# Loading the partial first and last blocks of x as a multiple of 16 rows and a rest

## The chip, the cores and the metric

The kernel runs on one core of one Trainium2 chip. The metric is the device time of one execution in microseconds (us). The spans in the profiles are some 1.7 us shorter than the device times of the same runs (445.9 against 447.63 for the kernel before).

## The reference

Two layers on x of 8 sequences x 4160 rows x 192 columns in float32: a causal convolution over 7 rows with softmax weights per head, then the channel mix of RWKV.

```python
def _attn_ref(x, weight):                       # x (8, 4160, 192), weight (8, 7)
    w = softmax(weight, axis=-1)                # cut: written out in the original
    x_pad = np.concatenate([np.zeros((B, 6, D)), x], axis=1)
    out = einsum('hk,bskhg->bshg', w, windows_of_7_rows(x_pad))
    return out.reshape(B, S, D)

def _moe_ref(x, mu_k, mu_r, w_k, w_v, w_r):     # w_k (192, 1024), w_v (1024, 192), w_r (192, 192)
    x_prev = x shifted down by one row
    xk = mu_k * x + (1.0 - mu_k) * x_prev
    xr = mu_r * x + (1.0 - mu_r) * x_prev
    k = np.maximum(xk @ w_k, 0.0)
    v = k * k @ w_v
    r = 1.0 / (1.0 + np.exp(-(xr @ w_r)))
    return r * v
```

## The kernel before

The rows of a sequence lie on the 128 partitions in blocks. A block gives 120 rows of output and needs 6 rows more ahead of them, so that one matmul with a banded 128x128 matrix (`toe`) is the convolution. `groups` says how many blocks are loaded at once. Two sequences (a pair) are worked on together, so a group is a tile `xb` of 128 partitions x blocks x 2 sequences x 192 columns.

```python
HALO = K - 1            # 6
BLK = 120
NBLK = -(-S // BLK)     # 35 blocks; the last has 86 rows of x
...
groups = []
for p in range(NPAIR):                      # 4 pairs of sequences
    blk0 = 0
    for nb, s, on_pe in (
        ((3, 0, True), (4, 1, True), (4, 2, True), (5, 3, True), (10, 4, False), (9, 6, False))
        if p == 0
        else ((10, 0, False), (10, 2, False), (10, 4, False), (5, 7, False))
    ):
        groups.append((p, blk0, nb, first_bundle[first_step[p] + s], on_pe))
        blk0 += nb
```

The first block of a sequence has no rows ahead of it: its 122 rows of x go to partitions 6 to 127, the other 6 hold zeros. The last block has 86 rows. Both are loaded by a DMA of their own, and the whole blocks of the group by a further one (the "main load" here). GpSimd (POOL) issues all of them, and they convert float32 to bfloat16 on the way.

```python
def load_x(g):
    p, blk0, nb, _, _ = groups[g]
    xb = xbs[g]
    for s in range(2):
        b = 2 * p + s
        lo, hi = 0, nb
        if blk0 == 0:
            lo = 1
            nc.gpsimd.dma_start(out=xb[HALO:P, 0, s, :], in_=x[b, 0 : P - HALO, :])
        t0 = blk0 * BLK - HALO
        if blk0 + nb == NBLK:
            hi = nb - 1
            r0 = t0 + hi * BLK
            nc.gpsimd.dma_start(out=xb[0 : S - r0, hi, s, :], in_=x[b, r0:S, :])
        nc.gpsimd.dma_start(
            out=xb[:, lo:hi, s, :],
            in_=bass.AP(
                tensor=x.tensor,
                offset=x.offset + (b * S + t0 + lo * BLK) * D,
                ap=[[D, P], [BLK * D, hi - lo], [1, D]],
            ),
        )
```

The start of the kernel, in the order in which POOL gets its work. The matrices `wk`, `wr` and `wv` are loaded by three, five and one DMAs.

```python
def prologue():
    ...
    load_x(0)          # group 0: two partial loads, two main loads
    masks_band()       # two short POOL instructions
    ...
    load_x(1)
    load_wk()
    load_x(2)
    load_wr()
    load_wv()
    ...
    for t in tails:
        nc.gpsimd.memset(t, 0.0)
    for c in range(0, len(chunks(0)), 2):
        conv_mm(0, c)  # the first convolution
    ...                # transposes of group 0, convolution of group 1
    x_tile(3, nc.vector)
    load_x(3)          # the fourth group
```

## Time and profile before

| what | kernel before |
|---|---|
| median of the first 3 runs | 447.46 us (447.34 to 447.76) |
| span in the profile | 445.9 us |
| TensorE busy | 433.8 us, 97% |
| POOL busy, instructions | 48.2 us, 70 |
| partial loads of x | 16: 8 of 122 rows, 8 of 86 rows |

The profiles call TensorE PE, VectorE DVE, ScalarE ACT, GpSimd POOL and SyncE SP. "Busy" is the time in which an engine works on an instruction; the chain of waits is the sequence of work, each piece released by the one ahead of it, that ended last. The prediction below shows the lines of the page and of the chain. The list of DMA queues of the kernel before gives packets, MB and the share of 16 engines:

```profile
q0 software_dynamic: 38224, 14.68, 29.1%
```

The timeline of TensorE gives start in us, length in us, engine, line, operation, output and inputs, shapes, count, and in brackets how long TensorE had been idle and what it waited for:

```profile
8.06 0.66 PE L250 MATMUL ps_c<-xb,toe 128*128 128x144 bf16 x8 [0.70 <-DMA xb<-in_x_dram]
...
23.82 0.98 PE L250 MATMUL ps_c<-xb,toe 128*128 128x240 bf16 x8 [1.20 <-DMA xb<-in_x_dram]
```

These are the two places where TensorE waits for x: the convolution of group 0 (3 blocks x 48 columns = 144) and that of the fourth group (5 blocks x 48 = 240). q0 is the queue of the DMAs that POOL issues.

### The profile page before, as it was taken

What the parts mean: (1) busy time and instruction counts of PE and PEld (TensorE: products, weight loads), DVE (VectorE), ACT (ScalarE), POOL (GpSimd) and SP (SyncE); (2) the same over time, 40 slices, a digit from 0 to 9 for tenths busy, and PEclk for the clock granted to TensorE, in tenths of its full rate; (3) what the DMA queues carried; (4) which work ended last, traced back from release to release, by engine and by line L of the source; (5) the groups of instructions that cost most, each with busy time, mean ns of one, the idle gap of its engine ahead of it and who ended that gap; (6) DMA issues with size and microseconds to landing.
All of it is one profiled execution on the core that took longest, in us unless ns stands there. A gap on an engine that the chain in (4) does not pass through costs nothing.

```text
span 445.9 us, 9765 instructions
## 1 busy us (share of the span) xinstructions
PE 433.8 (97%) x3937; PEld 304.5 (68%) x3937; DVE 387.8 (87%) x702; ACT 353.7 (79%) x465; POOL 48.2 (11%) x70
## 2 busy tenths in 40 slices
PE   7889999999999999999999999999999999999995
PEld 3555766776866776676676677667667677766685
DVE  4899799889988989889978998889988898999972
ACT  3878888888897788888888788888988778777771
POOL 8650001102020100012020000010200000000000
PEclk9999999999999999999999999999999999999999
DMA  8998759979497693295798493485964562522113
GB/s 89 150 186 157 187 146 160 162 188 197 122 206 194 128 197 103 80 202 138 154 209 167 121 216 114 111 118 160 197 160 115 162 153 80 111 72 71 64 47 114
DMA packets 133184, 63.64 MB, mean 143 GB/s; under 512 B 84723, under 2 KB 132883, under 8 KB 133139
## 3 DMA queue, kind: packets, MB, share of 16 engines
q1 hardware_dynamic: 94834, 48.28, 41.1%
q0 software_dynamic: 38224, 14.68, 29.1%
q8 instruction: 31, 0.51, 0.5%
q14 instruction: 15, 0.11, 0.1%
q10 hardware_dynamic: 80, 0.05, 0.0%
HBM read 29.39 MB, written 36.99 MB: 149 GB/s over the span
## 4 chain that ended last, share of the span: by engine, by line
PE 87%; DVE 3%; DMA 3%; ACT 3%; POOL 2%; issue 1%; DVEq 0%
PE ps_k L416 37%; PE ps_v L505 37%; PE ps_r L500 4%; PE ps_r L501 4%; PE ps_c L250 4%; DMA xb<-in_x_dram 1%; DMA wk<-in_moe_w_k_dram 1%; ACT y L286 1%; DVE k L476 1%; POOL xb L122 1%; ACT r_sb L522 1%; DVE o_sb L532 1%; PE ps_vt L505 0%; DVE xk L397 0%; ACT k_sb L457 0%
## 5 line engine op out<-in xcount | busy, mean ns | idle before, releaser
L457 ACT ACTIVATE k_sb<-ps_k 128x1024 bf16<-128x1024 f32 x260 | 245.9, 1035 | 13.0 <-PE ps_k L416 9.8
L416 PE MATMUL ps_k<-xk,wk 64*128 64x512 bf16 (+3 forms) x1056 | 191.6, 373 | 2.5 <-DVE xk L397 1.7
L505 PEld LDWEIGHTS <-k 128*128 128x128 bf16 x2048 | 170.9, 98 | 14.9 <-issue 0.7
L505 PE MATMUL ps_v<-wv,k 128*128 128x192 bf16 x2048 | 179.4, 246 | 0.6 <-ACT k_sb L457 0.6
L476 DVE TENSOR_TENSOR k<-k_sb 128x1024 bf16<-128x1024 bf16 x256 | 168.2, 686 | 10.2 <-ACT k_sb L457 9.1
L416 PEld LDWEIGHTS <-wk 64*128 64x128 bf16 (+1 forms) x1056 | 66.4, 96 | 102.0 <-issue 56.0
L532 DVE TENSOR_TENSOR o_sb<-ps_v,r_sb 128x768 f32<-128x768 f32 x64 | 61.2, 957 | 26.6 <-PE ps_v L505 26.2
L522 ACT ACTIVATE r_sb<-ps_r 128x768 bf16<-128x768 f32 x64 | 53.1, 829 | 24.8 <-PE ps_r L501 24.8
L286 ACT CAST y<-ps_c 120x480 bf16<-120x480 f32 (+6 forms) x84 | 38.4, 515 | 32.8 <-PE ps_c L250 32.8
L122 POOL DMA_DIRECT2D xb<-in_x_dram x36 | 32.2, 898 | 168.9 <-PE ps_k L416 95.2
L500 PE MATMUL ps_r<-wr,xr 128*128 128x192 bf16 x256 | 47.4, 246 | 0.2 <-DVE o_sb L532 0.2
L501 PE MATMUL ps_r<-wr,xr 128*128 128x192 bf16 x256 | 47.4, 246 | 0.0
L397 DVE TENSOR_TENSOR xk<-xk,yT 128x1024 bf16<-128x1024 bf16 (+1 forms) x66 | 36.2, 549 | 2.3
L397 DVE TENSOR_TENSOR xr<-xr,yT 128x1024 bf16<-128x1024 bf16 (+1 forms) x66 | 36.2, 549 | 2.3
L250 PE MATMUL ps_c<-xb,toe 128*128 128x480 bf16 (+4 forms) x144 | 30.9, 321 | 1.9 <-DMA xb<-in_x_dram 1.9
L355 DVE TENSOR_TENSOR d<-yT 128x1536 bf16<-128x1536 bf16 (+4 forms) x38 | 31.8, 837 | 0.1
L394 DVE TENSOR_SCALAR xk<-d,mu 128x1024 bf16<-128x1024 bf16 (+1 forms) x66 | 27.5, 416 | 1.2
L501 PEld LDWEIGHTS <-xr 128*128 128x128 bf16 x256 | 25.0, 98 | 3.9 <-issue 0.5
L500 PEld LDWEIGHTS <-xr 128*128 128x128 bf16 x256 | 25.0, 98 | 3.5
L394 DVE TENSOR_SCALAR xr<-d,mu 128x1024 bf16<-128x1024 bf16 (+1 forms) x66 | 27.2, 412 | 0.0
L289 ACT CAST y<-ps_c 120x480 bf16<-120x480 f32 (+6 forms) x45 | 20.3, 501 | 8.0 <-PE ps_c L250 8.0
L250 PEld LDWEIGHTS <-toe 128*128 128x128 bf16 x144 | 12.8, 98 | 3.6 <-issue 1.3
(57 smaller groups left out, 79.3 us busy)
## 6 DMA issues: line engine op xcount, KB each, us to landing
out_dram<-o_sb SPq DMA_DIRECT2D x62, 384.0 KB, 3.1
y_dram<-y SPq DMA_DIRECT2D x10, 900.0 KB, 7.0
xb<-in_x_dram POOLq DMA_DIRECT2D x14, 480.0 KB, 8.7
xb<-in_x_dram POOLq DMA_DIRECT2D x6, 432.0 KB, 7.8
xb<-in_x_dram POOLq DMA_DIRECT2D x10, 192.0 KB, 6.4
y_dram<-y SPq DMA_DIRECT2D x3, 450.0 KB, 4.1
y_dram<-y SPq DMA_DIRECT2D x1, 810.0 KB, 5.7
xb<-in_x_dram POOLq DMA_DIRECT2D x2, 384.0 KB, 7.1
```

What stands on the lines that cost most here:

```text
L250: nc.tensor.matmul(out=ps[:, :, :, i * G : (i + 1) * G], lhsT=toe[:, h, :], rhs=xbs[g][:, :nb, :, h * G : (h + 1) * G], start=True, stop=True,
L286: copy(out=yh[:, :, :, c0 : c0 + n], in_=ps[:BLK, :, :, 0:n])
L394: nc.vector.tensor_scalar(out=o, in0=d[:, sl, :L], scalar1=mu[:, i, part : part + 1], scalar2=None, op0=ALU.mult)
L397: nc.vector.tensor_tensor(out=o, in0=o, in1=yT[:, sl, c0 : c0 + L], op=ALU.add)
L416: nc.tensor.matmul(out=ps[:, i, f * L : (f + 1) * L], lhsT=wk[r, 0 if hi else 1, fs], rhs=xk[r, i if hi else 2, :L], start=start and f == ...
L457: nc.scalar.activation(out=k_sb, in_=ps.rearrange("p a b -> p (a b)"), func=AF.Relu)
L476: nc.vector.tensor_tensor(out=o, in0=i, in1=i, op=ALU.mult)
L500: nc.tensor.matmul(out=o, lhsT=hi, rhs=wr[:, 0, :], start=True, stop=False)
L501: nc.tensor.matmul(out=o, lhsT=lo, rhs=wlo, start=False, stop=True)
L505: nc.tensor.matmul(out=o, lhsT=k2s[s][:, f, t * P : (t + 1) * P], rhs=wv[:, f, :], start=(f == 0), stop=(f == NF - 1),)
L522: nc.scalar.activation(out=r_sbs[s, j], in_=ps, func=AF.Sigmoid)
L532: nc.vector.tensor_tensor(out=o_sb.rearrange("p (b t) d -> p b (t d)", b=2), in0=v_ps.pop((s, j)), in1=r_sbs.pop((s, j)), op=ALU.mult,)
```

## The change

Its intent is to give each partial load a row count that is a multiple of 16, so that its rows divide evenly over 16 DMA engines. The 122 rows become 112 and 10, the 86 rows become 80 and 6. The rest of a first block is issued after the main load, that of a last block at once.

```diff
             if blk0 == 0:
                 lo = 1
-                nc.gpsimd.dma_start(out=xb[HALO:P, 0, s, :], in_=x[b, 0 : P - HALO, :])
+
+                nc.gpsimd.dma_start(out=xb[16:P, 0, s, :], in_=x[b, 16 - HALO : P - HALO, :])
             t0 = blk0 * BLK - HALO
             if blk0 + nb == NBLK:
                 hi = nb - 1
                 r0 = t0 + hi * BLK
-                nc.gpsimd.dma_start(out=xb[0 : S - r0, hi, s, :], in_=x[b, r0:S, :])
+                n = (S - r0) // 16 * 16
+                nc.gpsimd.dma_start(out=xb[0:n, hi, s, :], in_=x[b, r0 : r0 + n, :])
+                nc.gpsimd.dma_start(out=xb[n : S - r0, hi, s, :], in_=x[b, r0 + n : S, :])
             nc.gpsimd.dma_start(
                 out=xb[:, lo:hi, s, :],
                 ...
             )
+            if blk0 == 0:
+                nc.gpsimd.dma_start(out=xb[HALO:16, 0, s, :], in_=x[b, 0 : 16 - HALO, :])
```

## The prediction

> **What bounds the kernel now.** I read the page first: busy shares, chain and queues.
>
> ```profile
> PE 433.8 (97%) x3937; PEld 304.5 (68%) x3937; DVE 387.8 (87%) x702; ACT 353.7 (79%) x465; POOL 48.2 (11%) x70
> ...
> PE 87%; DVE 3%; DMA 3%; ACT 3%; POOL 2%; issue 1%; DVEq 0%
> ```
>
> TensorE is busy for 97% of the span and is 87% of the chain that ended last. DMA and POOL, the only things that the change touches, are 3% and 2% of it (some 13 and 9 us). To see where these lie I read the chain of waits for the first 35 us; the columns are start in us, length in us, what.
>
> ```profile
> 1.58 0.72 POOL xb L116
> 2.30 0.74 POOL xb L122
> 3.03 0.56 POOL xb L116
> 3.59 0.71 POOL xb L122
> ...
> 4.98 1.43 POOL xb L122 x2
> 6.41 6.39 DMA wk<-in_moe_w_k_dram
> ...
> 13.08 0.52 POOL wr L167
> ...
> 14.31 0.77 POOL wv L170
> ...
> 17.03 6.65 DMA xb<-in_x_dram
> 23.68 0.14 issue
> 23.82 0.58 PE ps_c L250 x4
> ```
>
> So the start is a chain of POOL's DMA issues and of landings, up to the convolution of the fourth group of x (load issued at 17.03, landed 23.68, matmul at 23.82). From about 35 us on the chain is TensorE with short steps of ACT and DVE, and no load of x stands in it. The table of waits has one row in which TensorE waits for x:
>
> ```profile
> PE ps_c L250 <- DMA xb<-in_x_dram: 1.9, 2, 1.2
> ```
>
> Two waits, 1.9 us in all; the timeline of PE puts them at 8.06 (0.70) and 23.82 (1.20). After that no partial block comes near a deadline. The last partial blocks of the first pair land at 33.35 and are first read at 47.42; those of the second pair are issued from 102.59, land by 111.3 and are read at 153.85; the first blocks of the third pair are issued from 123.61, land by 136.2 and are read at 172.99. The slack is 14 to 42 us.
>
> **What the skill says.** The aim of the change is to give partial blocks a row count that is a multiple of 16. The Trainium skill, "DMA: Bandwidth & Descriptors", section "Why a DMA increments its semaphore by 16 and not by 1", says that the number of engines k is the largest number up to 16 that divides the slowest dimensions. By that rule 122 and 86 rows would run on 2 engines, 61 and 43 rows on each. The same section names an exception for DMAs issued from GpSimd: some direct copies get k = 16 with partitions/16, rounded up, on each engine. The trace decides which holds. The queue view for 205 to 225 us, in which two 86-row loads and two loads of 128x4 rows run, and that for 185 to 205 us, with two of 128x10 rows, say:
>
> ```profile
> q0 software_dynamic: 1280, 0.46, 19.4%
> ```
>
> ```profile
> q0 software_dynamic: 2592, 0.98, 44.2%
> ```
>
> The columns are packets, MB and share of 16 engines. The whole loads: 2 x 1280 rows leave 2592 - 2560 = 32 packets, 16 for each DMA (completions). The group with partial loads: 2 x 86 + 2 x 512 = 1196 rows leave 84 = 4 x 16 + 20. The 20 are 10 per 86-row load, and 96 - 86 = 10. Around 225 to 245 us, with two 122-row loads and two of 128x9, 2624 - (244 + 2304) = 76 = 4 x 16 + 12, so 6 per load, and 128 - 122 = 6. So I read that a partial load is already padded to a multiple of 16 and spread over 16 engines, 8 or 6 rows on each: the exception holds. The landings agree: the 86-row load issued at 23.84 lands 0.22 us behind the load ahead of it (29.04 after 28.82) and the 122-row one 0.25 us behind (33.60 after 33.35). With 43 or 61 rows on an engine at the 32 ns a row that a busy queue shows (1.28 us for the 40 rows per engine of a 128x5 load, 22.40 to 23.68), these would be 1.4 and 2.0 us.
>
> The same page, section "Rules for kernel authors", says to coalesce small transfers, because under 64 KB one pays mostly overhead; the change does the contrary. Here POOL takes 0.56 us to issue 122 rows and 0.53 us for 64 rows of wr, so the row count hardly matters. The page's section "Anatomy of one DMA" gives some 2.0 us fixed per DMA; here the first loads take 2.9 to 3.3 us from issue to landing, more than that.
>
> **Part by part.** Eight first blocks: 122 rows become 112 rows first and 10 rows after the main load. Eight last blocks: 86 become 80 + 6 back to back. The instruction lists show all else unchanged and in the same order: matmuls, DVE, ACT and SP alike, with 16 DMAs more on POOL.
>
> ```profile
> L116 POOL DMA_DIRECT2D xb<-in_x_dram x8: 557/567/718, 1.6 to 230.6; - x8
> ```
>
> 1. POOL: 16 issues x 0.55 us (567 and 557 ns are the medians of the two partial forms) = 8.8 us more busy, 48.2 to 57. 14 of the 16 come after 23 us, with POOL idle for tens of us around them and the slack above: worth 0.
> 2. Queue: bytes equal. Padding: 8 x (6 + 10) = 128 before; afterwards 112 and 80 need none, 10 and 6 need 6 and 10, again 128. Completions 16 x 16 = 256 more. q0 goes from 38224 to 38480 packets, 0.7% more of very small ones: no time.
> 3. Rows per engine: 8 become 7 + 1, 6 become 5 + 1. Gain 0.
> 4. The first group. Two extra issues stand in the chain above. The second main load (issue 3.59) goes out 0.55 us later, at 4.15, the 10 rows of the second sequence at 4.86, and all later issues (wk at 6.41) about 1.1 us later: 7.5. An issue is not a landing, though. wk's first packets start about 2.6 us after its issue, while the first load's start 1.8 us after (3.36 against 1.58), so 0.8 us of wk's time is queueing behind x. The queue itself starts later only by the main load's 0.55 us plus almost nothing for the 10 rows. I therefore take between 0.3 and 1.1 us, centre 0.5: x of group 0 lands at about 8.4 in place of 7.93, its convolution starts at 8.5 to 8.7, wk lands at 13.2 to 13.6 (12.80), the fourth group's convolution starts at 24.1 to 24.6 (23.82).
> 5. Waits on reused semaphores: a DMA waits for the one eight before it on POOL. With six DMAs instead of four in group 0 the first wk load now waits for the very first x load, landed at 4.90, and the others for loads of group 0 issued more than 5 us before. From wr on each pair is the same as before (wr still waits for wk, wv for the last wk, the fourth group for the third). No new stop.
>
> Sum: +0.5 us at the start, carried through a TensorE-bound stretch without slack, and 0 afterwards: 447.46 + 0.5 = **448.0 us**.
>
> **Rivals.** (a) *Partial loads run on two engines and hold up the queue; the change frees it.* For: the skill's general rule, and it is the evident intent. Against: the packet counts and the 0.22 us above. Even if true, only group 0 would gain: 122 rows in the first 5 us, at most some 1 us at the start, 446.5. (b) *POOL's issues bind fully*: each of the two issues costs its whole 0.55 us to the end, since wk, wr, wv and the fourth group follow each other on POOL: +1.1 us, 448.6. For: POOL makes up most of the chain up to 6.4 us. Against: the stops at 13.08 and 14.31 are for landings, not for POOL. (c) *Hidden wholly*: the extra issues vanish in the queue's backlog, which is nearly unbroken from 6 to 29 us: 447.5. Against: the second main load has no backlog in front of it; the queue pauses at 5.5. (d) *The 16 extra DMAs slow the output and transposing traffic late on*: the queues there are shared, but 256 tiny packets among 133184 are 0.2%, and late waits of TensorE on DMA are nil.
>
> **Range and chances.** Runs of the kernel before spread by 0.4 us. With (c) at the low end and (b) plus a delay of the 10-row landing at the high end I take 447.1 to 449.1 for 8 in 10. Two per cent is 8.9 us; nothing here reaches that, unless a late load came to lie on the path. Faster 0.01, same 0.98, slower 0.01.
>
> **What would show it.** Step 1: POOL busy near 57 us. Step 2: 38480 packets on q0; any other count refutes the padding rule. Step 4: the second wait of PE on x ends at 24.1 to 24.6, and the difference there equals the difference of the spans. Step 5: no POOL wait on a landing longer than before. The prediction is wrong if the small loads (10 and 6 rows) take far longer to land than the 112, so that the first convolution comes after 9 us, or if a wait of PE on x appears after 30 us.

## The result, and the profile after

| | before | after |
|---|---|---|
| median of 4 runs each | 447.40 us (447.19 to 447.76) | 448.60 us (448.24 to 449.27) |
| ratio, after over before | | 1.0028 (95%: 1.001 to 1.0045) |
| span in the profile | 445.9 us | 446.9 us |

A ratio is the mean time of one kernel's runs over that of the other's of the same rounds, so it isn't quite the ratio of the medians. The time is the same within 2%, and a little longer: by 1.2 us in the medians and 1.0 us in the spans of the profiles.

The page of the changed kernel, with the same lines as before:

```profile
PE 430.4 (96%) x3874; PEld 304.4 (68%) x3937; DVE 388.8 (87%) x702; ACT 353.7 (79%) x465; POOL 56.6 (13%) x86
...
q0 software_dynamic: 38480, 14.69, 29.2%
...
PE 86%; ACT 3%; DVE 3%; DMA 3%; POOL 2%; issue 2%; DVEq 0%
```

POOL has 16 instructions and 8.4 us more. TensorE's 430.4 us can't be set against 433.8: this trace lacks 63 matmul records (3874 against 3937, with the weight loads complete at 3937). The chain of waits of the changed kernel at its start (start, length, what):

```profile
3.03 0.52 POOL xb L134
3.55 0.56 POOL xb L117
4.10 0.74 POOL xb L125
4.85 0.50 POOL xb L134
...
7.53 0.55 POOL wk L163
8.07 0.51 POOL wk L164
8.58 5.93 DMA wk<-in_moe_w_k_dram
...
17.52 7.14 DMA xb<-in_x_dram
24.66 0.14 issue
24.80 0.58 PE ps_c L255 x4
```

The two issues of 10 rows (L134) stand in the chain with 0.52 and 0.50 us. What came after 5 us in the kernel before comes 1.1 us later: the first issue for wk from 6.41 to 7.53. Before the fourth group's load, the difference has shrunk to 0.5 (17.03 to 17.52); the load takes 0.49 us longer to land (7.14 for 6.65), and its convolution starts 0.98 us later. The timeline of TensorE of the changed kernel, with the two rows shown of before:

```profile
7.67 0.89 PE L255 MATMUL ps_c<-xb,toe 128*128 128x144 bf16 x8 [0.18 <-DVE toe L229]
...
24.80 0.98 PE L255 MATMUL ps_c<-xb,toe 128*128 128x240 bf16 x8 [1.75 <-DMA xb<-in_x_dram]
```

The first convolution starts 0.39 us *earlier*, and it no longer waits for x but for `toe`, which DVE makes. That is no gain of the change. In the profile of the kernel before, x of group 0 landed late, at 7.93; in a1, b1 and c2 (below), which load group 0 just as it does, x landed at 7.23, 7.28 and 7.13, and the first convolution started at 7.52 to 7.58. In the five profiles with group 0 split as in the change (after, a2, a3, b2, d0), x landed at 7.38 to 7.56, and it started at 7.53 to 7.69. The convolution of the fourth group starts 0.98 us later. The table of waits of the changed kernel (what waited, for what: us in total, times, longest) has one wait of the convolution for x in its first 36 us, instead of two:

```profile
PE ps_c L255 <- DMA xb<-in_x_dram: 1.7, 1, 1.7
```

From then on the two timelines run side by side at a constant distance: the matmuls that start at 32.59, 54.38, 134.48 and 440.22 us before start at 33.57, 55.35, 135.46 and 441.21. So in this pair of profiles all that the change does to the time it does in the first 25 us.

What does the delay do to the queue? In the kernel before, the loads of group 1 were issued from 4.92 us, here from 5.96. In their place the queue ran empty for a moment. The traffic of the kernel before between 6.9 and 7.7 us, and of the changed kernel between 7.0 and 7.8 us; the row "DMA" of the second is the busy share of the engines in tenths, in 40 slices of this window:

```profile
q0 software_dynamic: 181, 0.07, 94.8%
```

```profile
DMA  0000000000000000000000011484549893393331
...
q0 software_dynamic: 39, 0.01, 27.8%
```

In the changed kernel no packet moves in the first half of this window. The same row for 6.5 to 8.0 us, of the kernel before, of the changed kernel, and of a4 (below), which holds POOL up in group 0 without an additional DMA:

```profile
DMA  9749999239984793959396678967999999999999
```

```profile
DMA  9997532342100000000000000027698291301305
```

```profile
DMA  8464211010000000000000359259269010206011
```

Such an empty stretch, 0.4 to 0.9 us long, lies at about 7 us in the profiles of after, a2, a3, a4, b2 and d0, where POOL is held up in group 0, and in none of before, a1, b1, c2 and d2 (c1, d1 and d3 issue group 0 in quite another way). That it is what puts off the later loads is an inference from these windows.

The instructions of line 134, the 10-row loads (duration in ns as min, median, max; first and last start in us), and the traffic of the queue in the window from 205 to 225 us, both of the changed kernel:

```profile
L134 POOL DMA_DIRECT2D xb<-in_x_dram x8: 512/518/532, 3.0 to 233.6; - x8
```

```profile
q0 software_dynamic: 1312, 0.46, 19.6%
```

Issuing 10 rows takes 0.52 us, against 0.57 for 122: what costs is the issue, not the rows. The 1312 packets are the 1280 of before and 2 x 16 completions for the two additional DMAs. The rows themselves count the same as before, so nothing was gained for the DMA engines.

### The profile page after: what moved, and what is told of

It is laid out like the page before. It is cut to its first block, busy times and chain, and to the rows that moved or that the text cites. A ratio compares the mean times of both kernels' runs of the same rounds, so it can differ in the third digit from the quotient of the medians.

```text
span 446.9 us, 9728 instructions
## 1 busy us (share of the span) xinstructions
PE 430.4 (96%) x3874; PEld 304.4 (68%) x3937; DVE 388.8 (87%) x702; ACT 353.7 (79%) x465; POOL 56.6 (13%) x86
## 3 DMA queue, kind: packets, MB, share of 16 engines
q0 software_dynamic: 38480, 14.69, 29.2%
## 4 chain that ended last, share of the span: by engine, by line
PE 86%; ACT 3%; DVE 3%; DMA 3%; POOL 2%; issue 2%; DVEq 0%
PE ps_v L510 37%; PE ps_k L421 36%; PE ps_r L505 4%; PE ps_r L506 4%; PE ps_c L255 4%; ACT y L291 2%; DMA xb<-in_x_dram 2%; DMA wk<-in_moe_w_k_dram 1%; DVE k L481 1%; POOL xb L125 1%; ACT r_sb L527 1%; ACT y L294 1%; DVE o_sb L537 1%; PE ps_vt L510 0%; ACT k_sb L462 0%
## 5 line engine op out<-in xcount | busy, mean ns | idle before, releaser
L421 PE MATMUL ps_k<-xk,wk 64*128 64x512 bf16 (+3 forms) x994 | 188.1, 373 | 6.8 <-DVE xk L402 2.1
```

The costliest lines, as they stand in the source:

```text
L421: nc.tensor.matmul(out=ps[:, i, f * L : (f + 1) * L], lhsT=wk[r, 0 if hi else 1, fs], rhs=xk[r, i if hi else 2, :L], start=start and f == ...
```

## The experiments

The theory after the result: each of the two additional issues in group 0 holds up POOL by about 0.5 us at a time when the queue has nothing else to do, and that is the loss; the other 14 additional issues cost nothing, and a multiple of 16 gains nothing. Rivals: the loss comes from the late loads, from the odd sizes (10 and 6 rows) on the engines, or from POOL disturbing DVE.

One number sums up each profile: when the first matmul of the product with w_v starts (the first that writes `ps_v`, at 29.95 us in the kernel before), and how much of the span remains from there.

| kernel | median us (before in the same batch) | ratio, 95% | first `ps_v` | span | rest |
|---|---|---|---|---|---|
| before | | | 29.95 | 445.9 | 415.95 |
| after | 448.60 (447.40) | 1.0028, 1.001 to 1.0045 | 30.93 | 446.9 | 415.97 |
| a1, group 0 whole | 448.00 (447.68) | 1.0003, 0.9984 to 1.0022 | 30.29 | 446.2 | 415.91 |
| a2, only group 0 split | 448.66 (447.68) | 1.0021, 1.0004 to 1.0038 | 30.80 | 446.8 | 416.00 |
| a3, cuts off by one row | 448.61 (447.68) | 1.0013, 0.9995 to 1.003 | 30.93 | 446.9 | 415.97 |
| a4, POOL time only | 448.33 (447.68) | 1.0018, 0.9996 to 1.0039 | 30.36 | 446.3 | 415.94 |
| c1, group 0 in pieces | 455.09 (447.38) | 1.0161, 1.0138 to 1.0183 | 36.81 | 452.7 | 415.89 |
| c2, later loads in pieces | 449.06 (447.38) | 1.0034, 1.0013 to 1.0055 | 29.75 | 446.8 | 417.05 |
| b1, before, fourth group early | 447.41 (447.38) | 0.9992, 0.9972 to 1.0011 | 29.97 | 445.9 | 415.93 |
| b2, after, fourth group early | 448.84 (447.38) | 1.0026, 1.0007 to 1.0045 | 31.14 | 447.1 | 415.96 |
| d0, after again | 448.47 (447.61) | 1.0027, 1.0013 to 1.0041 | 30.69 | 446.6 | 415.91 |
| d2, after, two sequences in a DMA | 447.92 (447.61) | 1.0009, 0.9996 to 1.0022 | 31.04 | 447.0 | 415.96 |
| d1, before, two sequences in a DMA | 453.08 (447.61) | 1.0124, 1.011 to 1.0138 | 34.95 | 450.9 | 415.95 |
| d3, d1 with the fourth group early | 452.53 (447.61) | 1.0112, 1.0099 to 1.0125 | 35.18 | 451.2 | 416.02 |

The rest (good to 0.05 us, as the spans are given to a tenth) is 415.9 to 416.0 us in every profile but one. Whatever a kernel loses or gains here, it does in its first 31 us, and c2 is the exception that was made to be one. The first `ps_v` comes at 29.75 to 30.29 us in the four profiles with group 0 loaded as before (before, a1, b1, c2), and at 30.69 to 31.14 in the five with it split (after, a2, a3, b2, d0). The runs of one kernel differ by 0.4 us (b1) to 2.5 us (a4) from the lowest to the highest, and those of the kernel before by 2.6 us in the batch of a1 to a4. All kernels gave correct results.

### a1_group0_whole

The changed kernel, with group 0 loaded as before; the other 14 partial loads stay split.

```diff
-                nc.gpsimd.dma_start(out=xb[16:P, 0, s, :], in_=x[b, 16 - HALO : P - HALO, :])
+                r = HALO if g == 0 else 16
+                nc.gpsimd.dma_start(out=xb[r:P, 0, s, :], in_=x[b, r - HALO : P - HALO, :])
...
-            if blk0 == 0:
+            if blk0 == 0 and g > 0:
```

> The changed kernel, but the first group of x (the only one on the path) loaded as before, 122 rows in one DMA; the other 14 partial loads stay split. Theory (two extra issues of POOL ahead of wk and the later loads): the loss is gone, 447.2 to 447.8 us, ratio to before 0.999 to 1.001, and the fourth group's convolution starts at 23.6 to 24.1. Rival (16 extra DMAs or the new mapping of engine and semaphore cost all along): it stays at 448.2 to 449.3.

The ratio is 1.0003, and the fourth group's convolution starts at 23.86, as before (23.82). The median of 448.00 lies 0.2 us over the upper end of what was expected; the rest of the span is that of before, so the 14 late issues cost nothing here either. The profiled run did lose 0.3 us, between 23.86 and the first `ps_v` (30.29). In the same profile one `tensor_scalar` of DVE at 17.43 us took 1.06 us, where it takes 0.49 us in the kernel before (at 17.74). A POOL instruction ran beside it, and the last section comes back to this; that it is the cause of the 0.3 us is an inference. No run separates this rival, POOL disturbing DVE: the instruction in this place takes 0.49 to 1.06 us in the four profiles with group 0 as before, and 0.71 to 1.17 us in the five with it split.

### a2_group0_split

The reverse: the kernel before, with group 0 alone split.

```diff
-                nc.gpsimd.dma_start(out=xb[HALO:P, 0, s, :], in_=x[b, 0 : P - HALO, :])
+                r = 16 if g == 0 else HALO
+                nc.gpsimd.dma_start(out=xb[r:P, 0, s, :], in_=x[b, r - HALO : P - HALO, :])
...
+            if g == 0:
+                nc.gpsimd.dma_start(out=xb[HALO:16, 0, s, :], in_=x[b, 0 : 16 - HALO, :])
```

> The kernel before, with only the first group's partial load split (112 rows and 10 rows, two DMAs more). Theory: the whole loss, 448.2 to 449.3 us, ratio 1.002 to 1.004, fourth group's convolution at 24.5 to 25.1. Rival (the cost is in the later groups): 447.2 to 447.8.

Two of the 16 additional DMAs give the whole loss: 448.66, 1.0021, convolution of the fourth group at 24.67. Together with a1 this places the loss in group 0. Its packets on q0 are 38256 = 38224 + 2 x 16.

### a3_unaligned

The changed kernel with cuts that are no multiple of 16: 113 + 9 rows and 81 + 5 rows.

```diff
-                nc.gpsimd.dma_start(out=xb[16:P, 0, s, :], in_=x[b, 16 - HALO : P - HALO, :])
+                nc.gpsimd.dma_start(out=xb[15:P, 0, s, :], in_=x[b, 15 - HALO : P - HALO, :])
...
-                n = (S - r0) // 16 * 16
+                n = (S - r0) // 16 * 16 + 1
...
-                nc.gpsimd.dma_start(out=xb[HALO:16, 0, s, :], in_=x[b, 0 : 16 - HALO, :])
+                nc.gpsimd.dma_start(out=xb[HALO:15, 0, s, :], in_=x[b, 0 : 15 - HALO, :])
```

> The changed kernel with each cut moved by one row: 113 + 9 and 81 + 5 rows, so no piece is a multiple of 16, with the same count of DMAs. Theory (partial loads are padded to a multiple of 16 and spread over 16 engines whatever their rows): time as the changed kernel, 448.2 to 449.3; q0 packets 38736 = 38480 + 8 x 16 + 8 x 16, from 15 + 7 pads for 113 + 9 and 15 + 11 for 81 + 5. Rival (a row count that is not divisible runs on few engines): 113 and 9 rows run on 1 engine, 113 rows x 32 ns = 3.6 us on one engine, so the first convolution starts after 9 us and the kernel takes 450 us or more; packets then 38480.

By the rule of rival (a) all 113 rows would be on one engine (the 9 rows would be on nine, and not on one, as the expectation says). The first convolution starts at 7.69 (7.67 after), the first `ps_v` at 30.93 as after, and the median is that of after. But the fourth group's convolution starts at 24.30, and it waits for `k_sb`, the output of ACT, not for x, which landed at 24.16: the loss reached the same size by another path (see b1 and d0). The list of queues of this kernel:

```profile
q0 software_dynamic: 38736, 14.69, 28.6%
```

That is 256 more than after, and the rule read from the kernel before gives just this. Rows rounded up to 16 pad 113 by 15, 9 by 7, 81 by 15 and 5 by 11: 8 x 22 + 8 x 26 = 384 packets of padding, where after and before both have 128. So with one piece to a row the count of rows is rounded up, and whether it is a multiple of 16 makes no difference to the time that these runs could show (1.0013 here, 1.0027 and 1.0028 for the changed kernel, with overlapping intervals).

### a4_pool_time

The kernel before, with a POOL memset of about 0.5 us into an unused tile where the changed kernel issues its 10 rows. No DMA is added.

```diff
+    idle = const.tile([P, 512], BF16, tag="idle", name="idle")
...
+            if g == 0:
+                nc.gpsimd.memset(idle, 0.0)
```

> The kernel before, with a memset of a scratch tile on POOL (0.5 us) in the place of each of the two extra loads of the first group: POOL's time without the DMA. Theory (what counts is that POOL issues all later loads about 1.0 us later): 448.0 to 449.2 us, fourth group's convolution at 24.3 to 25.1, q0 packets 38224 as before. Rival (the small DMAs themselves, their place in the queue and the semaphores, cost): 447.2 to 447.8.

The median is 0.65 us over that of before, the fourth group's convolution starts at 24.23 (just short of the expected 24.3), and the packets are the 38224 of before. This points to POOL's time rather than the transfer, but the interval (0.9996 to 1.0039) takes in "no difference", and in its profile it is 0.4 us rather than 0.85 to 1.0: its first `ps_v`, 30.36, is hardly later than the 30.29 of a1. By itself it isn't conclusive.

### c1_group0_pieces

To make the cost large: the kernel before with each 122-row load of group 0 cut into 8 pieces, 14 DMAs more.

```diff
-                nc.gpsimd.dma_start(out=xb[HALO:P, 0, s, :], in_=x[b, 0 : P - HALO, :])
+                cuts = [HALO, *range(16, P + 1, 16)] if g == 0 else [HALO, P]
+                for u, v in zip(cuts, cuts[1:]):
+                    nc.gpsimd.dma_start(out=xb[u:v, 0, s, :], in_=x[b, u - HALO : v - HALO, :])
```

> The kernel before, with the first group's two partial blocks cut into eight pieces each (10 rows and 7 x 16): 14 DMAs more in the first group, seven times the dose of the change, the same bytes. Theory (each extra issue holds all later loads back by its 0.53 us once the queue's backlog is used up): 14 x 0.53 = 7.4 us, of which at most 1 us is hidden, so 453.8 to 455.3 us, with the fourth group's convolution at 30.2 to 31.5. Rival (the backlog hides issues, and what was seen is noise): under 451 us.

The chain of waits of this kernel:

```profile
1.57 4.11 POOL xb L118 x8
...
6.42 3.88 POOL xb L118 x8
...
30.66 0.60 PE ps_c L252 x4
```

Sixteen issues take 4.11 + 3.88 = 7.99 us, 0.50 each. The ratio of 1.0161 is worth 0.0161 x 447.4 = 7.2 us, or 0.51 us for each of the 14 additional ones, and the fourth group's convolution starts 6.84 us later. By the medians it is 7.7 us, 0.55 each. So in this part of the kernel nearly the whole time of an issue passes into the end: the first issue for wk goes out 6.75 us later (13.16 for 6.41), and the first `ps_v` comes 6.86 us later. At this dose x of group 0 itself lands late, at 13.14, and the first convolution waits 5.73 us for it, which it doesn't in the changed kernel. This gives the size of the term: an issue of a few rows costs its 0.5 us, not the half of it, and a2 with two of them (448.66 - 447.68 = 0.98 us) agrees.

### c2_later_pieces

The other half of the question: the same dose far from the start. The kernel before with all 14 partial loads outside group 0 cut into pieces of 16 rows, 82 DMAs more.

```diff
+                cuts = [HALO, *range(16, P + 1, 16)] if g > 0 else [HALO, P]
+                for u, v in zip(cuts, cuts[1:]):
+                    nc.gpsimd.dma_start(out=xb[u:v, 0, s, :], in_=x[b, u - HALO : v - HALO, :])
...
+                cuts = [*range(0, S - r0, 16), S - r0]
+                for u, v in zip(cuts, cuts[1:]):
+                    nc.gpsimd.dma_start(out=xb[u:v, hi, s, :], in_=x[b, r0 + u : r0 + v, :])
```

> The kernel before, with the 14 later partial blocks cut into pieces of 16 rows (82 DMAs more, over five times the late dose of the change) and the first group untouched. Theory (late loads have 14 to 42 us of slack): 447.2 to 448.2 us, ratio 0.999 to 1.001. Rival (extra DMAs cost wherever they lie, some 0.07 us each as 1.2 us over 16 would say): 452 to 454 us.

Both expectations missed: 449.06 us lies between them. The rest of the span is 417.05, so 1.1 us are lost late, by 82 DMAs. The trace tells where: a matmul at 54.38 in the kernel before is at 54.18 here, one at 67.50 is at 68.22. Between them lies this wait (table of waits of c2, 54 to 69 us):

```profile
DVE d L359 <- DMA yT<-y_dram: 2.6, 1, 2.6
```

The transposing read of y, which DVE needs for the second pair, took longer. The list of DMAs (last number: us from issue to landing), of c2 and then of the kernel before:

```profile
yT<-y_dram SPq DMA_TRANSPOSE x1, 9.1
```

```profile
yT<-y_dram SPq DMA_TRANSPOSE x1, 6.5
```

It lands at 58.47 in c2 and at 55.58 before. POOL's issues for the second pair, which wait for one another's landings, stretch to 44.59 us in c2, and their loads land as late as 54.07, beside the write of y and this read. In the changed kernel the same loads have landed by 40.90, ahead of the write at 43.82. That the overlap is what slows the read is an inference from these times. So the late loads have slack, but it isn't endless; the change uses 14 issues of it, and there it costs nothing.

### b1_before_x3_early and b2_after_x3_early

If the fourth group's load is the step that sets the end of the start, issuing it earlier should gain. In both kernels the fourth group was loaded ahead of wr and wv.

```diff
         load_x(2)
+        for c in range(0, len(chunks(0)), 2):
+            conv_mm(0, c)
+        x_tile(3, nc.vector)
+        load_x(3)
         load_wr()
         ...
-        for c in range(0, len(chunks(0)), 2):
-            conv_mm(0, c)
         ...
-        x_tile(3, nc.vector)
-        load_x(3)
```

> The kernel before, with the fourth group's load issued right after the third's and ahead of wr and wv (it was last, behind two waits for wk and two memsets). Theory (the start's end is set by that load's landing): it lands by 19 to 20 us in place of 23.7, the convolution's wait of 1.2 us vanishes, and the kernel takes 446.0 to 446.9 us. Rival (after it another wait takes its place, wv's landing or DVE): 447.2 to 447.8.

> The changed kernel with the same move. Theory: the two extra issues no longer end in a wait of TensorE for the fourth group, so its time is within 0.5 us of the moved kernel before: 446.1 to 447.3 us. Rival (the extra issues delay wk and the first group and these carry the loss): 1 us and more above the moved kernel before.

The gain did not come, and in both runs the rival's number did (447.41, and 1.4 us above it). In b1 the wait for x is gone (the fourth group's convolution runs at 22.61 and 23.47 us), but the time is that of before, 0.9992. The timeline of TensorE of b1:

```profile
29.97 2.80 PE L505 MATMUL ps_v<-wv,k 128*128 128x192 bf16 x32 [0.60 <-ACT k_sb L457]
```

In the kernel before this line stands at 29.95, released by the same ACT instruction. So a second path, through DVE and ACT to `k_sb`, ends at the same time as the one through x: before is a tie, to some tenths of a us (one `tensor_scalar` of this path took 0.90 us in b1 and 0.49 in before). In b2 the loss is still there, 1.0026, though x is early. The chain of waits of b2:

```profile
8.60 6.13 DMA wk<-in_moe_w_k_dram
...
31.14 1.89 PE ps_v L510 x21
```

The second path begins with wk, which waits behind the two additional issues just as the fourth group does (the issue of its last part starts at 8.60, and it lands at 14.73, for 7.47 and 14.03 in the kernel before). So the issues in group 0 hold up two paths at once, and moving the fourth group heals one of them.

### d0_after_again

The changed kernel once more, unedited, beside the d kernels.

> The changed kernel once more, unaltered, so that it stands on the same chip as the next three: 448.2 to 449.3 us.

It gives 1.0027 again. Its profile shows the tie from the other side. The fourth group's convolution starts at 24.00, close to before, and waits there for `k_sb` of ACT, not for x; and yet the first `ps_v` is at 30.69. Here the second path set the end. Its first matmul with w_k starts at 13.58 (13.01 in the profile of after), right behind the landing of the first part of wk at 13.54. The profile puts this wait down to a DVE instruction that ended at 13.55, so which of the two set it the trace doesn't tell.

### d2_after_both

If the number of issues costs and not the split, the split could be kept and the issues saved: each piece is loaded for both sequences of the pair by one DMA. Group 0 then has four DMAs as in the kernel before, and the rows per piece are multiples of 16 or the rests of 10 and 6.

```diff
+        def both(u, v, n, row):
+            nc.gpsimd.dma_start(
+                out=xb[u:v, n, :, :],
+                in_=bass.AP(tensor=x.tensor, offset=x.offset + (2 * p * S + row) * D,
+                            ap=[[D, v - u], [S * D, 2], [1, D]]))
...
+            both(16, P, 0, 16 - HALO)
...
+            both(0, n, hi, r0)
+            both(n, S - r0, hi, r0 + n)
         for s in range(2):
             ...                        # the main loads as they were
+        if blk0 == 0:
+            both(HALO, 16, 0, 0)
```

> The changed kernel with each piece of a partial block (112, 10, 80 and 6 rows) loaded for both sequences in one DMA: the cuts at multiples of 16 stay, the first group has 4 issues as in the kernel before in place of 6. Theory (the number of POOL's issues ahead of wk is the loss): 447.2 to 448.0 us, wk's last load lands at 13.7 to 14.3. Rival (the split itself, or the late landing of the 10 rows, is the loss): 448.2 to 449.3.

The median is 447.92, 1.0009, and the interval takes in 1; q0 has the 38224 packets of before. This agrees with the theory, but not cleanly. wk landed at 14.97 in the profile, later than expected, and the first `ps_v` was at 31.04; that profile is of a run of 448.72, while four of the six runs lie between 447.58 and 447.98. In it wk was issued at 6.55, hardly later than before (6.41), and the queue did not run empty, so what it lost, it did not lose to POOL's issues. Why this kernel has runs of two sorts is open, and the rival isn't excluded.

### d1_before_both and d3_both_x3_early

The same saving without the split: 122 and 86 rows for both sequences in one DMA, so that group 0 has one issue fewer than in the kernel before. d3 has the fourth group early as well, as in b1.

```diff
-                nc.gpsimd.dma_start(out=xb[HALO:P, 0, s, :], in_=x[b, 0 : P - HALO, :])
...
-                nc.gpsimd.dma_start(out=xb[0 : S - r0, hi, s, :], in_=x[b, r0:S, :])
...
+            both(HALO, P, 0, 0)
...
+            both(0, S - r0, hi, r0)
```

> The kernel before with each partial block loaded for both sequences in one DMA: one issue fewer in the first group. Theory of issues alone: 0.5 us less, 446.9. Theory with a tie (a second chain through DVE and ACT ends at the same time): no gain, 447.2 to 447.7.

> The last kernel with the fourth group's load ahead of wr and wv as well: neither x nor wk can hold TensorE up. Theory with a tie: the chain through DVE and ACT remains, the first v matmul starts at 29.5 to 30.0 us (29.95 in the kernel before), 447.0 to 447.7 us. If loads alone were the bound: 446.2 or less.

d1 met none of its expectations: 453.08 us, 1.0124. The instructions of these loads in d1, and the traffic of its queue from 205 to 225 us:

```profile
L114 POOL DMA_DIRECT2D xb<-in_x_dram x8: 1611/1848/2171, 1.6 to 318.6; - x8
```

```profile
q0 software_dynamic: 2448, 0.46, 23.5%
```

One issue takes 1.85 us, and the first load, issued at 1.57, lands at 9.95. In the window, 86 x 2 rows should give 172 packets; there are 1204 in their place (2448 less 1196 for the rows of all loads and 3 x 16 completions), and 1204 = 172 x 7. Each row piece comes with seven more packets, of 4 bytes. The whole run says the same. It has 49616 packets on q0: the 38224 of before, less 8 x 16 completions for the eight DMAs saved, less the 128 of padding, plus 11648, and 11648 = 4 x (122 x 2 x 7 + 86 x 2 x 7). The same instructions in d2, with 112, 80, 10 and 6 rows:

```profile
L114 POOL DMA_DIRECT2D xb<-in_x_dram x16: 583/628/828, 1.6 to 315.2; - x16
```

There the issue takes 0.63 us and no such packets appear (38224 in all). So the row count can matter, though not in the form in which the kernels use it: with two pieces to a row, 122 and 86 rows are cut up, and 112, 80, 10 and 6 are not. That a multiple of 16 is what decides isn't shown: 10 and 6 are none, and are spared; why is open. d3 has the same fault (452.53, 1.0112), which covers its question, so whether the tie of b1 can be beaten by saving an issue stays open.

What is shown, then, is that the loss comes from the additional issues in group 0 (a1, a2) and grows with their number (c1). That it is POOL's time, and not something else about the additional DMAs, is in part argued. For it speak c1, where the shift of POOL (6.75 us) and that of the end (6.86) agree, and the empty queue. The profiles of a4 and d2 lean the other way: wk's first issue 0.95 us later and the first `ps_v` 0.41 us in a4, 0.14 and 1.09 us in d2; their medians are on its side, but their intervals take in 1.

No kernel is clearly faster than the kernel before: b1, the best, equals it.

## Why the prediction was right, and where it was not

The time was predicted as 448.0 us within 447.1 to 449.1, the same within 2%; it is 448.6. By its own steps:

- **Step 1, POOL:** right. 56.6 us busy for "57", an issue 0.52 to 0.55 us. That the 14 late issues are worth 0 holds too: a1, and the constant rest of 415.9 to 416.0 us. (POOL isn't idle around all of them, as the step says: those of the first pair stand in one run of issues from 23.84 to 26.75.) c2 shows that their slack would end at some dose between 14 and 82 DMAs.
- **Step 2, the queue:** right to the packet, 38480, and a3 confirmed the rule behind it with 38736.
- **Step 3, rows per engine:** right, gain 0. a3 with odd cuts is as fast as after.
- **Step 4, the first group:** the place and the kind of loss were right, one term was mis-sized, and one path was left out. "x of group 0 lands at about 8.4" started from the late 7.93 of one profile: it landed at 7.38, which is 0.1 to 0.3 us later than in a1, b1 and c2, where the prediction had 0.5. The term that was mis-sized is the one taken "between 0.3 and 1.1 us, centre 0.5". It rested on wk's 0.8 us behind x, as if a late issue would only use up the backlog. But there was no backlog at 7.0 to 7.4 us: the queue stood empty. c1 measured 0.51 us per issue, so 1.0 for the two. With that term, 447.46 + 1.0 = 448.5. The path left out is the one through wk and `k_sb`. The fourth group's convolution came 0.98 us later, just outside "24.1 to 24.6", in the first profile of the changed kernel; in the second (d0) it came at 24.00, outside on the other side, and in a3 at 24.30, both times waiting for `k_sb`, while the first `ps_v` was 0.74 and 0.98 us late all the same.
- **Step 5, no new stop:** right. POOL's waits for landings of wk ahead of wr went from 1.5 to 1.1 us in two.
- **"The difference there equals the difference of the spans":** 0.98 and 1.0 in the one pair of profiles, but 0.18 and 0.7 in d0. That it held in the first is luck: there the path through x ended last.

Of the rivals, (a) is refuted by a3, (c) by a2 and c1, (d) by the constant rest. Rival (b), "each of the two issues costs its whole 0.55 us to the end", with 448.6, was the closest. What spoke against it in the prediction, the stops at 13.08 and 14.31 for landings, was no argument: the landings waited for were those of wk, which had been issued late themselves (the last part landed at 14.51 for 14.03, and at 14.73 to 15.00 in a2, a3, b2 and d0). Two paths, through the fourth group and through wk, ended together (b1), and the issues stood ahead of both (b2).

## What to carry to other kernels

Count the DMAs at the start of a kernel, not their rows: where each further load waits for POOL to issue it, an issue of 10 rows costs as much as one of 122, about half a microsecond, and here it counted nearly in full, as the queue had nothing waiting. Before changing row counts for the sake of even spreading, count packets in a short window, where padding and splitting can be read off exactly. Splitting a load that has tens of microseconds of slack cost and gained nothing with 14 more issues, and 1.1 us with 82; and before removing one wait, look whether a second path ends at the same time.

## What the Trainium skill lacked or had wrong

- **Which copies from GpSimd are spread over 16 engines.** "DMA: Bandwidth & Descriptors", section "Why a DMA increments its semaphore by 16 and not by 1", says that "some direct copies" are, with the partitions over 16 rounded up on each engine, and doesn't say which. Here all loads with one piece to a row were (122, 86, 113, 81, 10, 9, 6 and 5 rows: 38224, 38480 and 38736 packets to the packet), and the padding shows as packets. With two pieces to a row and 122 or 86 rows, each row piece came with seven packets more, of 4 bytes, and the issue took 1.85 us in place of 0.63 (d1 against d2). No page has this.
- **What an issue costs.** The same page, section "Issuing engines are not separate DMA queues", calls the time to initiate a DMA "usually small relative to the DMA itself". Here it is 0.50 to 0.57 us in the median for 5 to 122 rows, and a 10-row load landed 2.5 us after its issue at the earliest: 14 additional issues made the kernel 7.2 us longer (c1). The page has latencies to the first byte, but no figure for the time that an issue keeps GpSimd busy.
- **DVE beside GpSimd.** "SBUF — State Buffer", section "Who interferes with whom", says that `tensor_scalar` can contend with GpSimd for a shared port, and that one then blocks the other. The traces agree in part. A `tensor_scalar` of 128x1024 took at most 0.49 us while POOL was idle, and up to 1.17 us beside POOL's issues (1.40 in d1); but of those of 128x1024 and 128x512 that overlapped POOL's work only 4 of 20 were slow (over 0.5 us) in the kernel before, and 9 of 22 after. The page doesn't say what share to expect. No run tested it alone.
